# Moving the flush of GpSimd's FFN products behind two groups of top-k and rounding steps

## The chip, the cores and the metric

The kernel runs on one core of a Trainium2 chip. A core has five engines that run side by side, each with its own queue of instructions in program order: TensorE (PE: matmuls and transposes), VectorE (DVE), ScalarE (ACT), GpSimd (POOL) and SyncE (SP, which here issues DMA). An instruction waits at the head of its engine's queue until what it needs from other engines is done. The metric is the device time of one execution in microseconds (us); the time before the change is the median of three runs.

## The reference

Attention that keeps the 32 largest scores of each row, and then a gated feed-forward network (FFN), all in fp32:

```python
# q, k, v: (8, 8, 576, 64)
scores = (1 / sqrt(64)) * q @ k^T
kth = np.partition(scores, -32, axis=-1)[..., -32:-31]
scores = np.where(scores >= kth, scores, -1e9)
attn = exp(scores - max(scores)); attn = attn / (sum(attn) + 1e-9)
x = (attn @ v) as (8 * 576, 512)
# w_gate, w_val: (512, 1536); w_out: (1536, 512)
g = x @ w_gate
silu = g * (1 / (1 + exp(-g)))
out = (silu * (x @ w_val)) @ w_out          # (4608, 512)
```

## The kernel before

The work is cut into 160 units: a batch, a tile of up to 128 queries, and a pair of heads. The loop over n is a software pipeline: one iteration takes unit n through top-k, unit n-1 through the mask and exp, unit n-2 through the normalization, unit n-3 through the transposes and unit n-4 through attn @ v. Between these, pieces of the FFN are given out (`piece`), 256 rows of x at a time. During the first iterations the FFN's weights are loaded and rounded, piece by piece, through ScalarE, GpSimd and VectorE.

Rounding of one piece of weights is a generator of five stages. `weights` drives all pieces in a staggered way; `rounding(1)` is one step, which does a different stage for each of several pieces:

```python
    def rounded(src, dst):                      # one piece, 128 x 256
        ...
        nc.sync.dma_start(w[:], ...)                                        # L109
        yield
        nc.scalar.activation(size[:], high.bitcast(FP32), AF.Abs)           # L114
        nc.scalar.mul(low, low.bitcast(U32), 2.0**-29)                      # L116
        yield
        nc.gpsimd.tensor_scalar(size[:], size[:], HUGE, LEAST, ALU.min, ALU.max)   # L119, clamp
        yield
        nc.vector.tensor_scalar(bits, bits, 3, 0x3FFFFFFF, ...)             # L123, shift
        nc.gpsimd.tensor_tensor(bits, bits, low, ALU.add)                   # L126, add
        yield
        nc.vector.scalar_tensor_tensor(out=dst.bitcast(I32), in0=high, ...) # L129, merge

    def weights():
        ...
        lags = (5, 3, 2, 2, 0)
        for n in range(len(pieces) + lags[0]):
            for k, lag in enumerate(lags):      # in step n: merge of piece n-5, shift and add of
                upto(n - lag, len(lags) - k)    # piece n-3, clamp of piece n-2, load of piece n
            ready[0] = max(n - lags[0] + 1, 0)
            early[0] = lambda: [upto(n - 1, 2), upto(n, 2)]   # ScalarE's stage for the next two steps
            yield
        ...
        # then combinations of rows and columns of w_out, on GpSimd alone (L168, L176, L180, L185)
```

The top-k of a unit is one long row of VectorE instructions, a generator, so that other steps can be put between them. After it come the mask (GpSimd's large add, L349) and exp:

```python
        for r in range(rounds):                                     # in select(n)
            for t, hs in enumerate(heads):
                nc.vector.max(m[:, t, 8 * r : 8 * r + 8], cur[:, hs])           # L327
                yield
            if r < rounds - 1:
                for t, hs in enumerate(heads):
                    nc.vector.match_replace(rest[:, hs], ..., cur[:, hs], LOWEST)   # L331
                    yield
        ...
        nc.vector.tensor_scalar(e[:, hs], sc[:, hs], ...)           # L337

        nc.gpsimd.tensor_tensor(e[:, every], e[:, every], sc[:, every], ALU.add)    # penalize, L349

            nc.scalar.activation(e[:, hs], e[:, hs], AF.Exp, ...)   # weigh, L358

        nc.vector.reciprocal(tot[:, 0:nh], tot[:, 0:nh])            # normalize, L370
        yield
            nc.scalar.mul(e[:, hs], e[:, hs], tot[:, t : t + 1])    # L373

                nc.tensor.transpose(ps[0:kl, ...], e[:, k0 : k0 + kl], ident[:])    # turn, L385
```

An FFN product for gate or value is accumulated by TensorE (L468), evicted by ScalarE, and multiplied into h by GpSimd. The evictions are kept in the list `on_act`, the multiplications in `on_pool`; `flush` issues what a list holds:

```python
            def gate(ps, h=h):
                half = ffn.tile([P, 2, BLK], FP32, tag="gv", name="half_g", bufs=3)
                nc.scalar.activation(h[:], ps[:], AF.Tanh, scale=0.5)           # L493
                nc.scalar.mul(half[:], ps[:], 0.5)                              # L494
                nc.scalar.add(h[:], h[:], 1.0)                                  # L495
                on_pool.append(lambda: nc.gpsimd.tensor_mul(h[:], h[:], half[:]))   # L496

            def value(ps, h=h, s=s):
                val = ffn.tile([P, 2, BLK], FP32, tag="gv", name="val", bufs=3)
                nc.scalar.copy(val[:], ps[:])                                   # L500
                on_pool.append(lambda: nc.gpsimd.tensor_mul(h[:], h[:], val[:]))    # L501
```

One iteration of the loop:

```python
        def dve(k, beside=True):
            for _ in range(k * nh):                 # nh heads: 2, or 1 for the last tile of queries
                next(topk, None)
                due[0] += 5 / 11 if beside else 0
                if due[0] >= 1:
                    due[0] -= 1
                    rounding(1)
        ...
        flush(on_act)
        if 0 <= n - 1 < NU:
            penalize(n - 1)
        flush(on_pool)
        if 0 <= n - TURN < NU:
            run(turn(n - TURN))
        if n >= VALUES:
            finish_unit(n - VALUES)
        next(nxt, None)                             # score matmuls of unit n+1

        early[0]()
        if 0 <= n - 1 < NU:
            weigh(n - 1)
        run(nxt)                                    # their copies to SBUF (L297, L311)

        dve(2, beside=False)
        ...
        pieces(2)                                   # up to two FFN pieces on TensorE
        flush(on_act)
        flush(on_pool)
        dve(1)
        dve(1)
        next(norm, None)
        run(norm)
        next(ahead, None)
        pieces(1)
        next(ahead, None)
        dve(1)
        pieces(1)
        dve(2)
        run(topk)
        pieces(6)
```

`piece` itself flushes a list that holds more than one entry. A last pass over the program pins each engine's order to the order in which the kernel issues its instructions, so nothing is rescheduled afterwards.

Of the kernel before, what the change touches and what calls it, by code (L numbers as in the profile page):

```python
# [27 lines left out]
def kernel(  # L28
# [170 lines left out]
    def rounding(n):  # L199
        for _ in range(n):  # L200
            next(weight, None)
# [70 lines left out]
    def n_heads(qt):  # L272

        return 1 if qt == J else 2

    def scores(n):
        b, qt, hp = units[n]
        slab = preps[b * NHP + hp]
        sc = work.tile([P, 2 * S], FP32, tag="sc", name="sc", bufs=2)
        halves = [slice(0, D), slice(D, P)]  # L280
        half = S // 2

        def bank():
            return ps_t.tile([P, 512], FP32, tag="t", name="s")


        if qt == J:
            banks = [bank() for _ in range(2)]
            for i, ps in enumerate(banks):
                for d in halves:  # L290
                    k0 = R + i * half
                    nc.tensor.matmul(  # L292
                        ps[d, 0:half], slab[d, S + R : S + 2 * R], slab[d, k0 : k0 + half]
                    )
            yield
            for i, ps in enumerate(banks):
                nc.scalar.copy(sc[:, i * half : (i + 1) * half], ps[:, 0:half])  # L297
        else:
            q0 = S + 2 * R + qt * P
            banks = []  # L300
            for i in range(2):
                for hh, d in enumerate(halves):
                    ps = bank()
                    banks.append((i + 2 * hh, ps))
                    k0 = (1 - hh) * R + i * half
                    nc.tensor.matmul(  # L306
                        ps[:, 0:half], slab[d, q0 : q0 + P], slab[d, k0 : k0 + half]
                    )
            yield
            for i, ps in banks:  # L310
                nc.scalar.copy(sc[:, i * half : (i + 1) * half], ps[:, 0:half])  # L311
        state[n] = dict(sc=sc)

    def select(n):

        nh = n_heads(units[n][1])
        sc = state[n]["sc"]
        m = small.tile([P, 2, TOP_K], FP32, tag="m", name="m", bufs=2)
        heads = [slice(t * S, (t + 1) * S) for t in range(nh)]
        rest = work.tile([P, 2 * S], FP32, tag="rest", name="rest", bufs=1)  # L320
        e = work.tile([P, 2 * S], FP32, tag="e", name="e", bufs=4)
        state[n] |= dict(m=m, e=e, heads=heads)
        cur = sc
        rounds = TOP_K // 8
        for r in range(rounds):
# [5 lines that stand above are left out]
                    nc.vector.match_replace(  # L331
                        rest[:, hs], m[:, t, 8 * r : 8 * r + 8], cur[:, hs], LOWEST
                    )
                    yield
                cur = rest
        for t, hs in enumerate(heads):
            nc.vector.tensor_scalar(  # L337
                e[:, hs], sc[:, hs], m[:, t, TOP_K - 1 : TOP_K], FAR, ALU.is_lt, ALU.mult
            )

    def penalize(n):

        st = state[n]
        sc, m, e, heads = st.pop("sc"), st.pop("m"), st["e"], st["heads"]
        nh = len(heads)
        bias = small.tile([P, 2], FP32, tag="bias", name="bias")
        nc.gpsimd.tensor_scalar_mul(bias[:, 0:nh], m[:, 0:nh, 0], -scale)
        every = slice(0, nh * S)
        nc.gpsimd.tensor_tensor(e[:, every], e[:, every], sc[:, every], ALU.add)  # L349
        st["bias"] = bias  # L350

    def weigh(n):

        st = state[n]
        e, heads, bias = st["e"], st["heads"], st.pop("bias")
        tot = small.tile([P, 2], FP32, tag="tot", name="tot")
        for t, hs in enumerate(heads):
            nc.scalar.activation(  # L358
                e[:, hs], e[:, hs], AF.Exp, bias=bias[:, t : t + 1], scale=scale,
                accum_out=tot[:, t : t + 1],  # L360
            )
        nh = len(heads)
        nc.scalar.activation(tot[:, 0:nh], tot[:, 0:nh], AF.Identity, bias=eps[:])
        st["tot"] = tot

    def normalize(n):
        st = state[n]
        tot, e, heads = st.pop("tot"), st["e"], st.pop("heads")
        nh = len(heads)
        nc.vector.reciprocal(tot[:, 0:nh], tot[:, 0:nh])  # L370
# [4 lines that stand above are left out]
    def turn(n):  # L375

        last = units[n][1] == J
        e = state[n].pop("e")
        et = work.tile([P, 2 * J + 1, P], FP32, tag="et", name="et")
        for c0, cn in ((0, J), (J, 1)) if last else ((0, J), (J, 1), (J + 1, J)):  # L380
            ps = ps_t.tile([P, 512], FP32, tag="t", name="etps")
            kl = R if last and c0 == J else P
            for c in range(cn):
                k0 = (c0 + c) * P
                nc.tensor.transpose(ps[0:kl, c * P : (c + 1) * P], e[:, k0 : k0 + kl], ident[:])  # L385
            nc.scalar.copy(  # L386
                et[0:kl, c0 : c0 + cn, :],
                ps[0:kl, 0 : cn * P].rearrange("p (c j) -> p c j", c=cn),
            )
            if c0 == J:  # L390
                yield
        state[n]["et"] = et
# [55 lines left out]
    on_act, on_pool = [], []  # L448

    def flush(queue):  # L450
        while queue:
            queue.pop(0)()
# [205 lines left out]
    def fetch(n):  # L658

        b, qt, hp = units[n]  # L660
        i = b * NHP + hp
        if qt == 0:
            yield from prep(i)
        if qt == J and i + NHP < len(pairs):
            load(i + NHP)

    def pieces(n):
        for _ in range(n):
            if credit[0] >= 1:
                credit[0] -= piece()  # L670

    def run(steps):
        for _ in steps:
            pass

    def finish_unit(n):
        values(n)
        b, qt, hp = units[n]
        if qt == J and b + 1 < B:
            load_v((b + 1) * NHP + hp)  # L680
# [13 lines left out]
    for n in range(NU + VALUES):  # L694
        nh = n_heads(units[n][1]) if n < NU else 1
        topk = select(n) if n < NU else no
        over[n - 1] = normalize(n - 1) if 0 <= n - 1 < NU else no
        nxt = scores(n + 1) if n + 1 < NU else no
        ahead = fetch(n + 2) if n + 2 < NU else no
        norm = over.pop(n - 2, no)  # L700

        def dve(k, beside=True):

            for _ in range(k * nh):
# [6 lines that stand above are left out]
        if n >= NU - NHP:  # L711
            credit[0] = 8.0
        else:
            credit[0] = min(credit[0] + (4.45 if nh == 2 else 2.25), 8.0)
# [8 lines that stand above are left out]
        next(nxt, None)  # L723
# [4 lines that stand above are left out]
        run(nxt)  # L728

        dve(2, beside=False)  # L730
        if 2 <= n + 2 < NHP:
            load(n + 2)
        if n < NHP:
            load_v(n)
        pieces(2)
        flush(on_act)
        flush(on_pool)
        dve(1)
        dve(1)
        next(norm, None)  # L740
        run(norm)
        next(ahead, None)
        pieces(1)
        next(ahead, None)
# [5 lines that stand above are left out]
# [50 lines left out]
```

## Time and profile before

| | |
|---|---|
| time, median of 3 runs | 1882.18 us (1881.31 to 1884.37) |
| span of the profiled execution | 1879.8 us |
| mean granted TensorE clock | 0.956 of full speed |
| VectorE: MAX8, 128x576 (L327) | 745 ns each |
| VectorE: MATCH_REPLACE8, 128x576 (L331) | 741 ns each |
| GpSimd: add of e, mostly 128x1152 (L349) | 2392 ns each |
| GpSimd: product of h, 128x512 (L496, L501) | 1277 and 1293 ns each |
| TensorE: matmul of an FFN product, 128x256 (L468) | 381 to 384 ns each |

In the profile, busy time is the time in which an engine executes. A wait is idle time of an engine directly before an instruction, put down to the instruction of another engine that was seen to end last before it; this is inferred, and where several were waited for, the name can be that of a neighbour. "Lines" are lines of the kernel, L496 for example. A timeline gives start and duration in us, the engine, the line, the operation with its output and input, how many instructions were merged into the row, and in brackets the idle time in front of it. An average over the whole span hides that this kernel has a first stretch with weight rounding and a later one without.

### The profile page before, as it was taken

The numbers are of one execution on the slowest core, as the hardware profiler recorded it, in microseconds if no ns is written. First come the engines' busy times: TensorE is split into PE (matmuls) and PEld (weight loads), VectorE is DVE, ScalarE is ACT, GpSimd is POOL, SyncE is SP. The second block draws the span as 40 slices with busy tenths as digits, with TensorE's granted clock in tenths as the row PEclk, the third lists the DMA queues.
The fourth block names the chain that finished last, engine by engine and source line by source line (L and its number), as shares of the span: only waits on it lengthen the run. The fifth ranks groups of instructions, "written<-read, shape, count | busy, mean of one in ns | idle before, by whom it ended". The sixth has DMA issues, their size and how long they took to land.

```text
span 1879.8 us, 30848 instructions
## 1 busy us (share of the span) xinstructions
PE 1713.8 (91%) x10756; PEld 1413.8 (75%) x10756; DVE 1631.5 (87%) x3477; ACT 1210.3 (64%) x3015; POOL 1023.5 (54%) x1007
## 2 busy tenths in 40 slices
PE   3447789989999999899999999989999999899998
PEld 2335658878888878787788887878888878787877
DVE  7998889998999989997899989999899989999300
ACT  5666657666766676575667676766776667676531
POOL 4666655635455645564365655555546554556534
PEclk7668899989999999899999999999999999999989
DMA  7332212000300012000210003000210001000000
GB/s 187 96 85 79 62 35 57 10 3 3 83 7 12 1 40 52 12 1 13 54 37 1 12 3 82 8 12 1 63 29 12 1 14 49 16 1 12 1 12 12
DMA packets 111259, 59.67 MB, mean 32 GB/s; under 512 B 89088, under 2 KB 97280, under 8 KB 111104
## 3 DMA queue, kind: packets, MB, share of 16 engines
q1 hardware_dynamic: 109904, 57.41, 11.7%
q8 instruction: 85, 1.39, 0.3%
q14 instruction: 70, 0.57, 0.1%
q10 hardware_dynamic: 1200, 0.30, 0.1%
HBM read 48.23 MB, written 9.44 MB: 31 GB/s over the span
## 4 chain that ended last, share of the span: by engine, by line
PE 80%; DVE 6%; POOL 4%; ACT 3%; issue 3%; DMA 0%; POOLq 0%; ACTq 0%
PE f L468 39%; PE x_ps L554 8%; PE av L414 8%; PE etps L385 8%; PE s L306 6%; PE y_ps L554 5%; DVE m L327 2%; DVE rest L331 2%; PE s L292 2%; PE av L405 1%; POOL e L349 1%; PE kqps L261 1%; PE o_ps L514 1%; ACT e L358 1%; ACT sc L311 1%
## 5 line engine op out<-in xcount | busy, mean ns | idle before, releaser
L327 DVE MAX8 m<-rest 128x8 f32<-128x576 f32 x864 | 614.5, 745 | 2.2
L331 DVE MATCH_REPLACE8 rest<-m,rest 128x576 f32<-128x576 f32 x576 | 423.4, 741 | 0.0
L349 POOL TENSOR_TENSOR e<-e,sc 128x1152 f32<-128x1152 f32 (+1 forms) x160 | 382.7, 2392 | 59.5 <-DVE e L337 59.0
L468 PE MATMUL f<-xT,wg 128*128 128x256 f32 x1728 | 404.1, 384 | 0.0
L468 PE MATMUL f<-xT,wv 128*128 128x256 f32 x1728 | 397.9, 381 | 0.0
L468 PEld LDWEIGHTS f<-xT,wg 128*128 128x128 f32 x1728 | 323.9, 191 | 66.1 <-issue 23.4
L468 PEld LDWEIGHTS f<-xT,wv 128*128 128x128 f32 x1728 | 324.3, 190 | 55.6 <-issue 13.5
L496 POOL TENSOR_TENSOR h<-h,half_g 128x512 f32<-128x512 f32 x108 | 137.9, 1277 | 383.6 <-ACT h L495 378.3
L385 PE MATMUL etps<-ident,e 128*128 128x128 f32 (+1 forms) x1312 | 190.7, 291 | 134.6 <-POOL size L126 43.2
L327 DVE MAX8 m<-sc 128x8 f32<-128x576 f32 x288 | 205.2, 748 | 118.7 <-ACT sc L297 69.6
L385 PEld LDWEIGHTS etps<-ident,e 128*128 128x128 f32 (+1 forms) x1312 | 161.8, 149 | 166.1 <-POOL size L126 46.1
L358 ACT ACTIVATE e<-e,bias 128x576 f32<-128x576 f32 x288 | 222.0, 776 | 100.1 <-POOL e L349 100.1
L386 ACT COPY et<-etps 128x512 f32<-128x512 f32 (+1 forms) x448 | 185.0, 483 | 125.5 <-PE etps L385 123.8
L501 POOL TENSOR_TENSOR h<-h,val 128x512 f32<-128x512 f32 x108 | 139.6, 1293 | 159.9 <-ACT val L500 159.8
L373 ACT ACTIVATE e<-e,tot 128x576 f32<-128x576 f32 x288 | 211.5, 787 | 15.2 <-DVE tot L370 15.2
L331 DVE MATCH_REPLACE8 rest<-m,sc 128x576 f32<-128x576 f32 x288 | 211.6, 740 | 0.0
L337 DVE TENSOR_SCALAR e<-sc,m 128x576 f32<-128x576 f32 x288 | 173.9, 640 | 3.5
L414 PE MATMUL av<-et,v 128*64 128x128 f32 (+1 forms) x2560 | 175.6, 283 | 0.0
L306 PE MATMUL s<-kqT 64*128 64x288 f32 x1024 | 168.1, 444 | 3.9 <-ACT kqT L266 3.8
L311 ACT COPY sc<-s 128x288 f32<-128x288 f32 x512 | 163.8, 403 | 1.7 <-PE s L306 1.7
L493 ACT ACTIVATE h<-f 128x512 f32<-128x512 f32 x108 | 65.3, 604 | 147.8 <-PE f L468 147.8
L414 PEld LDWEIGHTS av<-et,v 128*64 128x64 f32 x2560 | 138.4, 146 | 23.3 <-issue 7.5
(71 smaller groups left out, 2036.4 us busy)
## 6 DMA issues: line engine op xcount, KB each, us to landing
kq_in<-in_k_dram SPq DMA_DIRECT2D x64, 128.0 KB, 2.8
v<-in_v_dram SPq DMA_DIRECT2D x32, 256.0 KB, 3.0
kq_in<-in_q_dram SPq DMA_DIRECT2D x62, 128.0 KB, 2.9
w<-in_moe_w_gate_dram SPq DMA_DIRECT2D x24, 256.0 KB, 2.7
w<-in_moe_w_val_dram SPq DMA_DIRECT2D x24, 256.0 KB, 2.7
w<-in_moe_w_out_dram SPq DMA_DIRECT2D x24, 256.0 KB, 2.6
out_dram<-o SPq DMA_DIRECT2D x40, 128.0 KB, 2.4
out_dram<-o SPq DMA_DIRECT2D x16, 256.0 KB, 2.4
```

The costliest lines, as they stand in the source:

```text
L306: nc.tensor.matmul(ps[:, 0:half], slab[d, q0 : q0 + P], slab[d, k0 : k0 + half])
L311: nc.scalar.copy(sc[:, i * half : (i + 1) * half], ps[:, 0:half])
L327: nc.vector.max(m[:, t, 8 * r : 8 * r + 8], cur[:, hs])
L331: nc.vector.match_replace(rest[:, hs], m[:, t, 8 * r : 8 * r + 8], cur[:, hs], LOWEST)
L349: nc.gpsimd.tensor_tensor(e[:, every], e[:, every], sc[:, every], ALU.add)
L358: nc.scalar.activation(e[:, hs], e[:, hs], AF.Exp, bias=bias[:, t : t + 1], scale=scale, accum_out=tot[:, t : t + 1],)
L373: nc.scalar.mul(e[:, hs], e[:, hs], tot[:, t : t + 1])
L385: nc.tensor.transpose(ps[0:kl, c * P : (c + 1) * P], e[:, k0 : k0 + kl], ident[:])
L386: nc.scalar.copy(et[0:kl, c0 : c0 + cn, :], ps[0:kl, 0 : cn * P].rearrange("p (c j) -> p c j", c=cn),)
L414: nc.tensor.matmul(av[hh * R : (hh + 1) * R, 0:ql], v_last[:, hh, :] if c == J else vt[:, hh, c, :], moving, start=last and c == 0, stop=c ...
L468: nc.tensor.matmul(ps[:, i, :], w[:, kc, m * P : (m + 1) * P], x[:, kc, :], start=(kc == 0), stop=(kc == KC - 1),)
L554: nc.tensor.matmul(ps, lhsT, T[i][m], start=m == 0, stop=m == MQ - 1)
```

## The change

The call that issues GpSimd's multiplications in the middle of an iteration moves down: from right behind the call that issues ScalarE's evictions to behind the next two groups of top-k steps, with the rounding steps that fall between them, and behind the normalization. No instruction is added, removed or altered. The multiplication needs the evictions to have ended, and GpSimd executes in order; placed later, it leaves GpSimd free for the rounding steps that are issued in between.

```diff
         pieces(2)
         flush(on_act)
-        flush(on_pool)
         dve(1)
         dve(1)
         next(norm, None)
         run(norm)
+
+        flush(on_pool)
         next(ahead, None)
         pieces(1)
         next(ahead, None)
```

## The prediction

> **What bounds the kernel now.** I read the page's totals and its 40 slices first, then the chain that ended last, and then asked where the change can act at all before looking at any stage closely.
>
> ```profile
> PE 1713.8 (91%) x10756; PEld 1413.8 (75%) x10756; DVE 1631.5 (87%) x3477; ACT 1210.3 (64%) x3015; POOL 1023.5 (54%) x1007
> ...
> PE   3447789989999999899999999989999999899998
> DVE  7998889998999989997899989999899989999300
> ...
> PE 80%; DVE 6%; POOL 4%; ACT 3%; issue 3%; DMA 0%; POOLq 0%; ACTq 0%
> ```
>
> TensorE carries 80% of the chain, VectorE is close behind (87% busy), GpSimd is half idle. One slice is 47 us. TensorE is full from about slice 8 on; in the first seven slices it is not, and VectorE is the fuller of the two. There the weights are being rounded beside the attention. The list of waits seems to offer much more:
>
> ```profile
> POOL h L496 <- ACT h L495: 378.3, 101, 15.8
> ```
>
> GpSimd sat 378 us idle in front of its first FFN product. That is the number that tempts; whether any of it counts depends on what stands behind the product in GpSimd's queue. I compared the two built programs engine by engine. VectorE, ScalarE, TensorE and the DMA queue keep their order. GpSimd keeps its order too, except in two places: five iterations where FFN work and rounding steps meet (159.6 to 246 us in the trace of before), and one iteration at 284 to 301 us where a product trades places with the combinations of w_out. Everywhere else GpSimd has no instruction between the old and the new place of the flush, so the program is the same. The first stretch against its neighbours, from the busy time by windows (us, then busy time and count of PE, PEld, DVE, ACT, POOL, then granted clock and DMA):
>
> ```profile
> 119.70:159.60 39.90, 17.49 (x112) 14.37 (x113) 39.90 (x98) 27.27 (x73) 24.96 (x34) 0.70 0.32 93
> 159.60:246.00 86.40, 66.73 (x366) 54.39 (x364) 70.04 (x159) 53.00 (x133) 52.35 (x64) 0.90 0.18 54
> 246.00:284.00 38.00, 36.32 (x209) 20.74 (x206) 35.36 (x73) 23.61 (x62) 21.12 (x20) 1.00 0.20 49
> ```
>
> Before the FFN starts, VectorE is busy all 39.9 us: three iterations in 39.9 us, 13.3 each. In the five that follow it is idle 86.40 - 70.04 = 16.36 us. The waits of VectorE, then of TensorE, in 158 to 250 us (total, times, longest):
>
> ```profile
> DVE size L123 <- POOL size L119: 16.4, 5, 3.8
> ```
>
> ```profile
> PE etps L385 <- POOL size L126: 11.1, 2, 6.6
> PE etps L385 <- POOL size L119: 6.6, 1, 6.6
> PE etps L385 <- issue: 1.9, 1, 1.9
> ```
>
> All of VectorE's idle time is one wait, once per iteration: the shift of a rounding step waits for GpSimd's clamp. The timelines of GpSimd and then VectorE in the first of the five show why:
>
> ```profile
> 159.84 2.64 POOL L349 TENSOR_TENSOR e<-e,sc 128x1152 f32<-128x1152 f32 x1
> 167.23 1.27 POOL L496 TENSOR_TENSOR h<-h,half_g 128x512 f32<-128x512 f32 x1 [4.75 <-ACT h L495]
> 168.46 0.75 POOL L126 TENSOR_TENSOR size<-size,w 128x256 int32<-128x256 int32 x1
> 169.29 0.40 POOL L119 TENSOR_SCALAR size<-size 128x256 f32<-128x256 f32 x1
> ```
>
> ```profile
> 166.07 0.40 DVE L129 SCALAR_TENSOR_TENSOR wo<-w,size 128x256 int32<-128x256 int32 x1
> 169.72 0.29 DVE L123 TENSOR_SCALAR size<-size 128x256 int32<-128x256 int32 x1 [3.25 <-POOL size L119]
> 178.99 2.17 DVE L129 SCALAR_TENSOR_TENSOR wo<-w,size 128x256 int32<-128x256 int32 x1
> 181.08 1.36 DVE L123 TENSOR_SCALAR size<-size 128x256 int32<-128x256 int32 x1
> ```
>
> GpSimd finishes e at 162.5, and the next thing in its queue is the product of h, which waits until 167.23 for ScalarE (exp, score copies, tanh, half, plus one). The rounding add and clamp, whose inputs have been there since 164.6, stand behind it; VectorE needs that clamp at 166.4 and gets it at 169.7. TensorE's transposes are a second victim: they wait for ScalarE's normalization (L373), which waits for VectorE's reciprocal; in the second iteration that reciprocal stands behind the stall (188.30), the normalization starts at 188.49, the transposes at 189.37. The label "POOL size" on those waits is the profile's guess at the releaser.
>
> **What the Trainium skill says.** "Perfetto Trace Analysis", section Sequencer Loop: an engine's instructions are pushed into its queue and wait there for their semaphores; so a waiting head holds what is behind it. The trace agrees: 4.75 us of idle GpSimd with ready rounding work behind. "GPSIMD Engine Reference", section Specifications: GpSimd shares its SBUF interfaces with VectorE and contends with VectorE instructions that have two SBUF inputs or run in a 2-port mode. The trace agrees: the merge L129 (two inputs) took 2.17 us instead of 0.40 at 178.99, ending 0.3 after GpSimd's e add; the shift L123 after it took 1.36 instead of 0.29, ending with the next product; MAX8 on one input keeps its 0.75 beside them. "TensorE: Matmul & The Clock Gate", section Part 1: gaps bring a slower TensorE clock. Seen: nine transposes took 2.15 us after the 6.61 us gap, 1.15 without one.
>
> **The change, part by part.** Nothing is added or removed. Per iteration the gate product (L496, 1.27 us) moves behind one or two rounding steps (by the fraction 5/11 per VectorE step: one in the first and third iteration, two in the others). I followed each iteration by hand with the durations above: GpSimd add 0.73 and clamp 0.40 to 0.6, product 1.27, e 2.62; VectorE MAX 0.66, replace 0.73, merge 0.33, shift 0.20 from start to start; ScalarE's plus one done 4.0 to 4.7 us after e.
> - First (stall 3.25): the first clamp is done at 165.9, so the second shift runs at 166.4. But here the product comes after one rounding step: it holds GpSimd from 167.2 to 168.5, the second clamp is done at 169.7, the third shift wants it at 168.4. Left: 1.3. Gained: 1.95.
> - Second (3.21): two steps ahead, no wait left. The port block of 178.99 shrinks by about 0.4, a new one comes in: the product lies at 184.0 to 185.3, under the third merge, about 1.1. Gained: 2.5.
> - Third (3.01): one step ahead; the second add lies behind the product and then under the third merge, 0.9 left. Gained: 2.1.
> - Fourth (3.78): two ahead; product 212.6 to 213.9, merge blocked 0.5. Gained: 3.3.
> - Fifth (3.11): two ahead, merge blocked 0.4. Gained: 2.7.
>
> Sum 1.95 + 2.5 + 2.1 + 3.3 + 2.7 = 12.55 us of the 16.4. Can TensorE follow? It has 86.40 - 66.73 = 19.7 us idle in the stretch, and with the reciprocals earlier by 5 to 13 us the transposes of the third to sixth iteration come at 184.0, 199.1, 212.9 and 227.6 by the same walk, where they stood at 189.4, 204.1, 223.8 and 240.9. Gaps of 1 to 4 us stay, so TensorE isn't the bound there. From 251 us on, every engine has its inputs about 12.5 us earlier and the rest, in unchanged order, shifts as one block.
> - The sixth place, 284 to 301 us: the value product waits 4.08 us for ScalarE at 290.3; two L185 (1.44 together) and one L176 (1.27) can now run in that idle time, so the next e add comes 2.7 earlier, and a VectorE wait of 0.99 and a port block of 0.9 fall away. TensorE is full there (50.00 of 50 us from 300 to 350), but in 350 to 400 it has 42.73 against VectorE's 49.38, so a VectorE lead may be cashed. I count 0.5 of 1.9.
>
> Total: 12.55 + 0.5 = 13 us; 1882.2 - 13 = 1869 us, 0.7%.
>
> **The rivals.**
> - *The 378 us come back.* For it: the size of the number. Against it: 360 of them (378.3 less 18.1 in the five iterations) stand where GpSimd's order doesn't change, and behind them waits nothing that another engine lacks. It would mean 1840 or less; I give it 1%.
> - *Another wait takes the place.* GpSimd's product now comes later in the middle of the rounding steps, where it can block VectorE by the queue (one step ahead) or by the shared SBUF interfaces. I have counted 1.3 + 1.1 + 0.9 + 0.5 + 0.4 = 4.2 for it; if each iteration pays a whole 1.27 product on top, the gain drops to 7 and the time to 1875.
> - *TensorE becomes the bound of the stretch.* For it: its 66.7 busy us, partly at a low clock, in a stretch shrunk to 74. Against it: shorter gaps raise the clock and shorten that work. If it held, 3 to 5 us of the gain would go: 1873.
> - *All of the stall comes back*, if the blocks fall beside the merges: 1865.
>
> **Range and chances.** The centre is 1869. The lowest credible is the whole stall plus the whole sixth place, 16.4 + 1.9: 1864. The highest takes the second rival in full: 1876. The scatter of before (1881.31 to 1884.37) lies inside. Two percent is 37.6 us, more than twice all that can be reached; slower by 2% has no mechanism.
>
> **What would show it.** In the profile after: VectorE's wait for the clamp falls from 16.4 to about 2 us in five pieces or fewer; the five iterations take about 74 us instead of 86.4; the merges' mean in that stretch stays above 0.5 us by blocks; TensorE's waits in front of the transposes fall from 19.6 to under 10; the wait of the product for ScalarE over the whole span stays near 360 us. Later stretches should look the same, 12 to 13 us earlier. I'd be wrong if ScalarE's evictions, unblocked, are late for another reason (weight loads, a clock of TensorE that falls with the new rhythm), or if the shift isn't kept because a later stage was set by something that doesn't move.

## The result and the profile after

| | before | after |
|---|---|---|
| time, median of 6 runs | 1882.99 us (1881.31 to 1884.37) | 1870.79 us (1866.99 to 1873.33) |
| ratio, 95% interval | 1 | 0.9933 (0.9920 to 0.9946) |
| span of the profiled execution | 1879.8 us | 1870.2 us |

12.2 us less, where 13 were predicted. The totals of the page hardly show it; among the slices, VectorE's fourth to sixth (141 to 282 us) rise from 8 to 9:

```profile
PE 1715.9 (92%) x10756; PEld 1415.0 (76%) x10756; DVE 1632.2 (87%) x3477; ACT 1210.1 (65%) x3015; POOL 1023.4 (55%) x1007
...
DVE  7999999998999989997999989999999989999300
```

The same five iterations in the busy time by windows (columns as in the prediction):

```profile
159.70:233.80 74.10, 65.54 (x368) 52.38 (x367) 72.10 (x159) 52.80 (x133) 52.85 (x64) 0.95 0.19 62
```

They take 74.1 us instead of 86.4. VectorE is busy for 72.10 of them, 2.06 more than the 70.04 of before, and idle for 2.0 instead of 16.4. The waits of VectorE, then of TensorE, in 158 to 240 us, and then GpSimd's largest wait over the whole span:

```profile
DVE size L123 <- POOL size L119: 2.0, 2, 1.0
```

```profile
PE etps L385 <- POOL size L126: 4.5, 2, 3.0
PE etps L385 <- issue: 4.2, 2, 3.4
```

```profile
POOL h L496 <- ACT h L495: 360.6, 97, 15.8
```

Two waits of 1.0 are left of five of 3.0 to 3.8. TensorE's waits in front of the transposes halve with them, from 19.6 to 8.7 us (4.5 + 4.2). And 360.6 of GpSimd's 378.3 us of waiting are still there: the time fell without them. The queue of GpSimd in the first of the five iterations, and VectorE's merges (L129) and shifts (L123) beside it:

```profile
164.93 0.73 POOL L126 TENSOR_TENSOR size<-size,w 128x256 int32<-128x256 int32 x1 [2.35 <-ACT sc L311]
165.75 0.40 POOL L119 TENSOR_SCALAR size<-size 128x256 f32<-128x256 f32 x1
167.34 1.28 POOL L496 TENSOR_TENSOR h<-h,half_g 128x512 f32<-128x512 f32 x1 [1.19 <-ACT h L495]
168.58 0.92 POOL L126 TENSOR_TENSOR size<-size,w 128x256 int32<-128x256 int32 x1
169.47 0.40 POOL L119 TENSOR_SCALAR size<-size 128x256 f32<-128x256 f32 x1
```

```profile
168.09 0.81 DVE L129 SCALAR_TENSOR_TENSOR wo<-w,size 128x256 int32<-128x256 int32 x1
169.90 0.29 DVE L123 TENSOR_SCALAR size<-size 128x256 int32<-128x256 int32 x1 [1.00 <-POOL size L119]
...
184.68 1.45 DVE L129 SCALAR_TENSOR_TENSOR wo<-w,size 128x256 int32<-128x256 int32 x1
```

The first clamp now ends at 166.15 instead of 169.7, and the product starts when it did before, 167.3. But only one rounding step stands ahead of it here, so the second add and clamp lie behind it and VectorE still waits 1.0. In the second iteration (last row) there is no wait; a merge takes 1.45 us instead of 0.41, beside the product. Over the five iterations a merge takes 0.63 us on average, before it was 0.53.

How far the gain is carried on is read from one and the same instruction in both timelines, a reciprocal after the stretch, first before, then after:

```profile
249.56 0.15 DVE L370 RECIPROCAL tot<-tot 128x2 f32<-128x2 f32 x1
```

```profile
237.35 0.15 DVE L370 RECIPROCAL tot<-tot 128x2 f32<-128x2 f32 x1
```

The 160 reciprocals, one per unit, make a ruler. "Shift" below is the start of such a one less its start in the kernel before. After the change it is +0.1 until 165 us, -12.2 at 237, -14.2 at 298 (the sixth place), within 0.7 of -12.2 from 332 to 743, and then moves in steps of 0.5 to 1.7 us in both directions, to -13.4 and at the end -9.5.

### The profile page after: what moved, and what is told of

The parts are those of the page before. It is cut to its first block, busy times and chain, and to the rows that moved or that the text cites. A ratio compares the mean times of both kernels' runs of the same rounds, so it can differ in the third digit from the quotient of the medians.

```text
span 1870.2 us, 30845 instructions
## 1 busy us (share of the span) xinstructions
PE 1715.9 (92%) x10756; PEld 1415.0 (76%) x10756; DVE 1632.2 (87%) x3477; ACT 1210.1 (65%) x3015; POOL 1023.4 (55%) x1007
## 4 chain that ended last, share of the span: by engine, by line
PE 80%; DVE 7%; ACT 4%; POOL 3%; issue 2%; DMA 0%; POOLq 0%; ACTq 0%; SPq 0%
PE f L468 39%; PE x_ps L554 8%; PE av L414 8%; PE etps L385 8%; PE s L306 6%; PE y_ps L554 5%; DVE m L327 3%; DVE rest L331 2%; PE s L292 2%; PE av L405 1%; ACT e L358 1%; PE kqps L261 1%; PE o_ps L514 1%; POOL e L349 1%; ACT sc L311 1%
## 5 line engine op out<-in xcount | busy, mean ns | idle before, releaser
L496 POOL TENSOR_TENSOR h<-h,half_g 128x512 f32<-128x512 f32 x108 | 137.9, 1276 | 372.3 <-ACT h L495 360.6
```

## The experiments

The theory to be tested: VectorE sets the pace of the five iterations; GpSimd's product holds VectorE, either through the queue (clamps behind it) or by holding the merges beside it, which the prediction puts down to the shared SBUF interfaces; TensorE and everything later only follow. The rivals: a part of the gain lies elsewhere (sixth place, the other products); TensorE's late transposes set the pace; it is enough that the product isn't first.

For each run I take the five iterations from the first MAX8 of one to the first of the sixth and split them into VectorE's idle time, the time of its 22 merges (from the start of each to the start of VectorE's next instruction, without idle time), and the rest. Worked out from the timelines:

| | stretch, us | idle | 22 merges | the rest |
|---|---|---|---|---|
| before | 86.5 | 16.4 | 10.3 | 59.8 |
| after | 74.2 | 2.0 | 12.4 | 59.8 |
| the later place in the five iterations only | 74.2 | 2.0 | 12.4 | 59.8 |
| the later place in the sixth place only | 86.5 | 16.4 | 10.3 | 59.8 |
| reciprocal first | 86.4 | 16.5 | 10.1 | 59.8 |
| no product | 68.5 | 0 | 8.8 | 59.8 |
| behind one group | 77.7 | 6.5 | 11.4 | 59.8 |
| two steps ahead in all five | 73.6 | 0 | 13.8 | 59.8 |
| behind three groups | 74.1 | 0 | 14.4 | 59.7 |
| two steps ahead, half a product | 70.7 | 0 | 11.0 | 59.8 |
| two steps ahead, product in two halves | 73.5 | 0 | 13.7 | 59.8 |

The rest is the same in all. Idle time and merges are the whole account of the differences; what each run did to them is told below. The split comes from one profile of each kernel, the times from 4 to 14 executions.

### The five iterations alone, and the sixth place alone

```diff
         flush(on_act)
+        if n > 15:          # five iterations alone; n <= 15 for the sixth place alone
+            flush(on_pool)
-        flush(on_pool)
         dve(1)
         dve(1)
         next(norm, None)
         run(norm)
+        flush(on_pool)
```

> The later flush in the iterations with weight rounding alone (n up to 15); from n = 16 on the flush stands where it stood before. Theory (the five iterations carry the gain; the sixth place gives a lead of 2 us that is taken back within 50 us): VectorE's wait for the clamp falls from 16.4 to 2.0 us as in the changed kernel, the reciprocals after the stretch come 12.2 us earlier and stay so, without the 14.2 seen at 298 us; time 1870 to 1872. Rival (the sixth place or the 96 other products carry a part): the shift after 400 us is 11 or less and the time 1873 or more.

Measured: 1871.39 us, ratio 0.9936 (0.9924 to 0.9948). Clamp wait 2.0 us, shift -12.34 from 250 to 380 us, no -14.2. As expected, with the whole of the gain: the changed kernel has 0.9933.

> The complement: the old place up to n = 15, the later one from n = 16 on, which changes GpSimd's order in the one iteration at 284 to 301 us. Theory: no shift before 300 us, about 2.0 us of lead for VectorE there, gone by 350 us, time 1882 to 1884, the same as before. Rival (the lead is cashed in the stretch at 350 to 400 us where TensorE is less busy): 1.5 to 2 us are kept, 1881. If the waits of GpSimd for ScalarE counted anywhere else, the time would fall by more than 2.

Measured: 1882.83 us, ratio 1.0004 (0.9996 to 1.0012). The shift is +0.2 up to 300 us, -1.8 at 311, -1.2 at 322 and +0.2 at 345. So the sixth place gives VectorE a lead of 2 us and the iterations after it take it back. In the changed kernel it is seen who takes it; VectorE's timeline:

```profile
303.93 1.42 DVE L327 MAX8 m<-sc 128x8 f32<-128x576 f32 x2 [0.51 <-ACT sc L311]
...
326.72 1.42 DVE L327 MAX8 m<-sc 128x8 f32<-128x576 f32 x2 [1.58 <-ACT sc L311]
```

VectorE comes early and waits 0.51 and 1.58 us for the score copies, which follow a TensorE without a gap (busy 50.00 of 50 us from 300 to 350). The later place gains nothing outside the five iterations. What the product's other waits would be worth if they were removed is not shown by this, as GpSimd's order stays the same there.

### Who passes the gain on

```diff
         flush(on_act)
         flush(on_pool)
+        if 11 <= n <= 15:
+            next(norm, None)
         dve(1)
         dve(1)
         next(norm, None)
```

> The kernel before, with VectorE's reciprocal moved ahead of the first of the two groups of top-k and rounding steps in the five iterations, so that it no longer stands behind the stall; the flush stays. It sets ScalarE's normalization and with it TensorE's transposes free about 3 us earlier in three of the five. Theory (VectorE's own stalls set the pace and TensorE only follows): VectorE still waits 15 to 17 us for the clamp, TensorE's waits before the transposes fall from 19.6 to about 11, the time falls by 0 to 1 us, 1882. Rival (TensorE's late transposes set the pace): the time falls by 6 to 9 us, to 1875.

Measured: 1884.09 us, ratio 1.0010 (1.0001 to 1.0018). The reciprocals of the five iterations come 3.3 to 10 us earlier and the shift right after the stretch is -0.1. VectorE's waits, and the transposes of TensorE that follow an idle time:

```profile
DVE size L123 <- POOL size L119: 16.5, 5, 3.8
```

```profile
186.34 1.38 PE L385 MATMUL etps<-ident,e 128*128 128x128 f32 x9 [3.27 <-issue]
204.07 2.15 PE L385 MATMUL etps<-ident,e 128*128 128x128 f32 x9 [5.25 <-issue]
...
237.83 2.15 PE L385 MATMUL etps<-ident,e 128*128 128x128 f32 x9 [6.49 <-issue]
```

The transposes that stood at 189.37 and 240.94 start at 186.34 and 237.83, three microseconds earlier as meant. The time doesn't fall, it is 0.1% up if anything: this decides against the transposes as what sets the pace. My number for TensorE's waits missed: they fall from 19.6 to 16.6 us, not to 11. Released early, TensorE is done early and waits again, 5.25 and 6.49 us, for the next iteration. A follower's waits move; they don't go away.

### The product taken out

```diff
-                on_pool.append(lambda: nc.gpsimd.tensor_mul(h[:], h[:], half[:]))
+                if now[0] > 15: on_pool.append(lambda: nc.gpsimd.tensor_mul(h[:], h[:], half[:]))
```

> The kernel before without GpSimd's gate product in the five iterations (six multiplications of h by half the gate are left out, so the first 256 rows are computed without that factor); ScalarE still evicts everything. Theory: the wait for the clamp goes to 0, and no product lies under a merge; the whole 16.4 us come back, 1865 to 1867, which is 4 us more than the changed kernel, the price of its two waits of 1.0 and of its blocked merges. Rival (another limit in the stretch, TensorE or ScalarE, takes over once the stalls are gone): the shift after the stretch is no larger than the 12.2 us of the changed kernel.

Measured: 1866.46 us, ratio 0.9915 (0.9900 to 0.9929); the stretch is 18.0 us shorter, the shift after it -17.8. The busy time by windows of the stretch:

```profile
159.80:228.30 68.50, 63.83 (x371) 51.92 (x369) 68.50 (x159) 52.57 (x133) 45.13 (x58) 0.98 0.22 67
```

VectorE is busy in every one of 68.50 us, and TensorE, idle for 4.7, isn't in the way even then. So nothing else limits this stretch down to 68.5. It is 1.6 more than the 16.4 I expected: the merges are shorter too, 8.8 against 10.3 before, 1.2 of that in one of them, the 2.17 us merge of the prediction, here 0.95. Before, it lay under the add of e and ended 0.29 us after it. Here the add has ended at 175.27, before the merge starts at 175.83; the merge now lies under a value product and ends 0.28 after that one.

### How far behind

```diff
         flush(on_act)
-        flush(on_pool)
         dve(1)
+        flush(on_pool)
         dve(1)
```

> Half the move: the flush stands behind the first of the two groups. In the built order the product then comes behind no rounding step in the first of the five iterations and behind one in the other four. Theory (what counts is how many rounding steps GpSimd has done when it comes to the product): the stall of the first iteration stays at 3.2 us, the other four keep about 1.0 each as the first and third do in the changed kernel; VectorE's wait for the clamp is 6.5 to 8 us, the shift after the stretch -5 to -9 us, time 1873.5 to 1877.5. Rival (it is enough that the product no longer comes first): 12 us as in the changed kernel.

Measured: 1871.81 us, ratio 0.9945 (0.9933 to 0.9958). The waits for the clamp:

```profile
DVE size L123 <- POOL size L119: 6.5, 5, 3.2
```

They are 3.25 us in the first iteration, 1.00 in each of the next three and 0.29 in the fifth. The stretch is 8.8 us shorter, inside the range; the time, 9.8 us below that of before in the same session, is 1.7 below the range given for it. Being no longer first isn't enough: the first iteration has no rounding step ahead of the product and gains nothing (its length changes by 0.01 us). That is read from the trace. By the times alone this kernel isn't clear of the changed one in the same session (0.9934, 0.9922 to 0.9946).

The other direction: in the first and third iteration one group later, so that all five have two rounding steps ahead:

```diff
         dve(1)
         dve(1)
         next(norm, None)
         run(norm)
-        flush(on_pool)
+        if n not in (11, 13):   # left out altogether up to n = 15 for "three groups"
+            flush(on_pool)
         next(ahead, None)
         pieces(1)
         next(ahead, None)
         dve(1)
+        flush(on_pool)
         pieces(1)
```

> The changed kernel, but in the first and third of the five iterations the product waits for one group more, so that two rounding steps stand ahead of it in all five. Theory: the two waits of 1.0 us for the clamp go to about 0.1, the merge behind them is no longer blocked (0.4 and 0.2); shift after the stretch -13.5 to -15 us against -12.2, time 1868 to 1870. Rival (the product only moves its hold to a later merge or clamp of the same iteration): -12 to -12.5.

Measured: 1869.85 us, ratio 0.9940 (0.9926 to 0.9954), shift -12.6. The theory's shift was wrong and the rival's nearly right; the time lies in the theory's range, but the rival's lies too near to be told apart by it. No wait for the clamp is left, but GpSimd's product and VectorE's merge in the first iteration now read:

```profile
167.93 1.28 POOL L496 TENSOR_TENSOR h<-h,half_g 128x512 f32<-128x512 f32 x1
```

```profile
168.03 1.46 DVE L129 SCALAR_TENSOR_TENSOR wo<-w,size 128x256 int32<-128x256 int32 x1
```

The merge starts 0.1 after the product and ends 0.28 after it. Of 2.0 us of idle time saved, 1.4 went into merges.

> The later place (behind three groups) in all five iterations: three rounding steps ahead of the product in the second and fourth, two in the others. Theory: no wait for the clamp, but the product of 1.28 us still lies beside a run of merges every 2.7 us or so, so it blocks another merge instead of the third; shift -13 to -15 us, time 1868 to 1870.5. Rival (later is always better): more than 15.5, near the 18.0 of the kernel without the product.

Measured: 1868.85 us, ratio 0.9929 (0.9916 to 0.9941), shift -12.5, below my range of 13 to 15 and far from the rival's 15.5, though the time is in my range: no wait, merges 14.4. The changed kernel, in the same session:

> The changed kernel once more on the same chip as the three others, to compare them with it: 1869 to 1872 us, shift after the stretch -12.2.

Measured: 1870.44 us, ratio 0.9934 (0.9922 to 0.9946), stretch 74.2 as in its first profile. Its shift was -12.3 when the stretch ended, -10.7 at 258 and 334 us, and -13.3 at 456. The three kernels can't be told apart by their times.

### What the merge waits for

Two steps ahead in all five, and the product halved in width, once with the other half left out, once with it behind the next clamp:

```diff
-                on_pool.append(lambda: nc.gpsimd.tensor_mul(h[:], h[:], half[:]))
+                k = 1 if now[0] <= 15 else 2
+                on_pool.append(lambda: nc.gpsimd.tensor_mul(h[:, 0:k], h[:, 0:k], half[:, 0:k]))
```

> The kernel with two rounding steps ahead of the product in all five iterations, and the product cut to its first half (256 of 512 columns; the other half of the first 256 rows' gate factor is left out in these iterations). Theory (the product holds VectorE's two-input merge for as long as it runs): VectorE's merges in the five iterations, 13.8 us with the whole product and 8.75 without one, come to 10.5 to 11.5, the stretch to 70.3 to 71.5 us against 73.6. Rival (what holds the merge is a fixed cost of each meeting): 13 or more.

Measured: 1865.26 us, ratio 0.9906 (0.9893 to 0.9920), stretch 70.7, merges 11.0. The half product and the merge of the first iteration (in this kernel the product is L497):

```profile
167.97 0.74 POOL L497 TENSOR_TENSOR h<-h,half_g 128x256 f32<-128x256 f32 x1
```

```profile
168.08 0.91 DVE L129 SCALAR_TENSOR_TENSOR wo<-w,size 128x256 int32<-128x256 int32 x1
```

As expected: with the product 0.54 us shorter (0.74 instead of 1.28) the merge is 0.55 shorter (0.91 instead of 1.46), and it again ends 0.28 after the product. Against 8.8 without a product, the 22 merges cost 2.2 more with half of it and 5.1 more with all of it; a part of both is the merge under the add of e, which takes 1.65 and 2.19 us in these two kernels and 0.95 without a product.

```diff
+                if now[0] <= 15:
+                    on_pool.append(lambda: nc.gpsimd.tensor_mul(h[:, 0:1], h[:, 0:1], half[:, 0:1]))
+                    halves.append(lambda: nc.gpsimd.tensor_mul(h[:, 1:2], h[:, 1:2], half[:, 1:2]))
...
         dve(1)
-        flush(on_pool)
+        flush(halves if n not in (11, 13) else on_pool)
         pieces(1)
-        dve(2)
+        dve(1)
+        flush(halves)
+        dve(1)
```

> Nothing left out: the same kernel with the product split in two halves of 256 columns, each behind a clamp of its own (in the fifth iteration both stand together). Theory: half a product fits more nearly into the time between a clamp's end and the next merge, so the merges cost 10.5 to 12 us, the stretch takes 70.5 to 72 us, the time is 1866 to 1868. Rival (the hold is only cut in pieces, each under a merge of its own): merges 13.5 or more, stretch 73.5, time as with two steps ahead, 1869 to 1870.

Measured: 1870.14 us, ratio 0.9931 (0.9917 to 0.9944), stretch 73.5, merges 13.7: the rival's numbers. (The kernel's lines L497 and L498 are the two halves.) GpSimd's two halves in the second iteration, and VectorE's merges:

```profile
183.96 0.73 POOL L497 TENSOR_TENSOR h<-h,half_g 128x256 f32<-128x256 f32 x1
...
186.33 0.74 POOL L498 TENSOR_TENSOR h<-h,half_g 128x256 f32<-128x256 f32 x1
```

```profile
184.07 0.90 DVE L129 SCALAR_TENSOR_TENSOR wo<-w,size 128x256 int32<-128x256 int32 x1
...
186.56 0.79 DVE L129 SCALAR_TENSOR_TENSOR wo<-w,size 128x256 int32<-128x256 int32 x1
```

Each half meets a merge and holds it to its own end. The idea that half a product would fit into the gap was wrong, because GpSimd's add and clamp already fill most of the time between a shift and the next merge: the clamp ahead of the first half ended at 184.0, and the merge was due at 184.07.

## Why the prediction was right

It was right in its centre (1869 against 1870.8), and the runs let its steps be judged one by one. The mechanism held; how near the number came owes something to errors that cancel.

- *Only six iterations change.* Shown: the five carry the whole gain (0.9936 alone), the sixth nothing (1.0004 alone).
- *The stall is a clamp behind a waiting product, and VectorE sets the pace.* Shown: without the product, and also with the whole product behind two steps, the idle time is 0; without it the stretch is 18.0 us shorter; with the reciprocals freed but the stall left, nothing is gained.
- *The sum by iterations.* The predicted gains were 1.95, 2.5, 2.1, 3.3 and 2.7; the starts of the iterations give 1.85, 2.22, 1.84, 3.53 and 2.87, together 12.3 against 12.55. The kinds of loss were right as well: two waits (1.0 each, counted as 1.3 and 0.9), and a merge under the product in the second iteration (1.45 instead of 0.41, so 1.04, counted as 1.1). Two terms were wrong: the merge under the add of e was to shrink by 0.4 and took 2.17 us as before, and the first iteration's merge beside the product (0.81 instead of 0.40) wasn't counted. The single gains were off by 0.1 to 0.3 in both directions, so the sum is better than its parts.
- *TensorE can follow.* Right: its waits before transposes fell to 8.7, "under 10"; the transposes of the third to sixth iteration had been put at 184.0, 199.1, 212.9 and 227.6 and start at 184.6, 200.1, 214.2 and 228.6, a little late each time.
- *The sixth place, 0.5 of 1.9.* Wrong in the part that was counted: the lead was there (2.0) and was given back whole by 345 us, to waits for TensorE's scores, before the stretch in which it should have been cashed.
- *The rivals.* The 378 us did not come back: the wait in front of the product fell by 15.1 us in the five iterations (18.05 to 2.94) and, as labelled, by 17.7 in all. "Another wait takes the place" is what kept 4 of the 16.4 us: 2.0 idle and 2.1 in longer merges. The full form of it, 1.27 on top in each iteration, didn't happen.
- *From 251 us on everything shifts as one block.* Right to about 740 us in the first profile, apart from the sixth place, and not beyond; in the profile of the changed kernel taken again only to 250 us (-10.7 at 258). The shift moves in steps. One of them can be followed in these two profiles of one program. TensorE's transposes near 1618 us and the FFN matmuls after them, and the busy time by windows, first:

```profile
1618.61 2.16 PE L385 MATMUL etps<-ident,e 128*128 128x128 f32 x9 [3.01 <-issue]
...
1624.90 3.72 PE L468 MATMUL f<-xT,wg 128*128 128x256 f32 x16
```

```profile
1610.00:1630.00 20.00, 15.23 (x94) 12.36 (x95) 19.17 (x43) 14.76 (x40) 6.14 (x4) 0.83 0.08 27
```

and again:

```profile
1617.70 1.38 PE L385 MATMUL etps<-ident,e 128*128 128x128 f32 x9 [3.01 <-issue]
...
1621.43 3.72 PE L468 MATMUL f<-xT,wg 128*128 128x256 f32 x16
```

```profile
1609.10:1629.10 20.00, 15.24 (x106) 12.29 (x107) 19.19 (x43) 15.99 (x42) 7.12 (x5) 1.00 0.08 27
```

The gap in front is 3.01 us in both, but the granted clock was 0.83 in one and 1.00 in the other, nine transposes took 2.16 and 1.38 us, and from the transposes to the FFN matmuls it was 6.29 and 3.73 us, 2.6 more. A second such step, behind a gap of 2.04 us at 1713, adds 1.4. Together they are most of the 4.8 us between the two spans (1870.2 and 1865.4 us, with the same stretch of 74.2). Why the clock fell in one and not in the other is open. I put the scatter of the times (1867.0 to 1873.3) down to such steps; no run tested it. It was not in the prediction's working, only in its range.

My own later theory did worse than the prediction: that two rounding steps ahead would save 2 us more. It took the queue for the cost and forgot that a product out of the queue's way lies beside VectorE's merges.

## What to carry to other kernels

A long wait in this profile was worth what stood behind it in the queue: compare the order of instructions first, and count only the places where something that another engine lacks stands behind the waiting one. When a GpSimd operation is moved out of the way, look where it lands in time, and count the VectorE instructions there that a GpSimd operation was seen to hold: here the merges with their two SBUF inputs, and under the value product the shift (1.36 us instead of 0.29, in every run). There the same microsecond can be paid again as a longer instruction, which no list of waits shows. Such a trade is seen only if idle time and durations are added up together.

## What the runs showed that I had not expected

- From two groups on, where the product stands matters little to VectorE: 2.0 idle and 12.4 in merges, 0 and 13.8, 0 and 14.4, 0 and 13.7 in two halves; 73.5 to 74.2 us for the stretch in all four, against 77.7 behind one group. Only less of it (70.7) or none (68.5) is cheaper.
- A merge that starts 0.1 us after a product doesn't run beside it at a lower rate; it ends 0.28 us after it, whether the product takes 1.28 us or 0.73 (merges of 1.46 and 0.90 to 0.91). The same holds for all 100 merges between 158 and 250 us of the twelve profiles that started while an add or a product of GpSimd ran: each ended 0.28 or 0.29 us after it. A merge with no GpSimd operation beside it took 0.40 to 0.42 us. MAX8 and MATCH_REPLACE8 kept their times in all runs (0.73 to 0.76 us in the stretch): the rest of the account is 59.7 to 59.8 us everywhere.
- TensorE's granted clock fell at a gap of 3.01 us in one execution and not at the same gap in another of the same kernel. The two profiles are 4.8 us apart, over a third of the effect that was to be measured.
